# One load for the first 512 tokens, wider first matmuls and a new order of work in a gated attention + MLP kernel

## The chip, the core and the metric

The kernel runs on one core of a Trainium2 chip. A core has five engines that run at the same time and meet only at semaphores: TensorE (PE in the profile: matmuls; PEld: its weight loads), VectorE (DVE), ScalarE (ACT), GpSimd (POOL) and SyncE (SP), which here only issues transfers. Transfers between the chip's memory (HBM) and the core's on-chip memory (SBUF) run on 16 DMA engines; SP and ScalarE each put them into a queue of their own. TensorE writes to PSUM, eight banks of 128 partitions x 512 float32 columns.

The metric is the device time of one execution in microseconds (us).

## The reference

Input x has 2048 tokens of 512 features. The output is `g * a + (1 - g) * b` per token, where `g` is a sigmoid of x times a weight vector, `a` an attention branch and `b` an MLP branch:

```python
x = A_x
g = _sigmoid((x * gate_w).sum(-1, keepdims=True))
a = _A_ref(x, A_wq, A_wk, A_wv, A_wo, A_beta)   # 4 segments of 512 tokens, 32 heads of width 16
b = _B_ref(x, B_w_gate, B_w_up, B_w_down)       # (gelu(x w_gate) * (x w_up)) w_down, width 1792
return g * a + (1 - g) * b
```

In each segment the attention branch computes causal softmax attention within the segment, and reads a memory matrix that collects phi(k)^T v over the segments before it, with `phi(t) = t + 1 if t > 0 else exp(t)`. A sigmoid of beta mixes the two per head.

## The kernel before

**Tiling.** The four segments are called s = 0 to 3. For each, x is needed transposed (`xT`: four blocks of 128 features on the partitions, 512 tokens as columns), and from it come K and Q (four output blocks `K{s}_{t}`, `Q{s}_{t}`, each a sum over four feature blocks), V (four token tiles `V{s}_{tile}`), the MLP's gate (`G{s}_{ft}`, 14 blocks) and up projections (`U{s}_{ft}`, 14 blocks), attention scores (`qk...`, 20 steps with an exponential on ScalarE behind each), probabilities times V (`pv...`), and the down projection with the attention's output projection (`D...`, `R...`). A name such as `K0_2.1` is the second piece of a task's matmuls. Results leave PSUM by a copy on ScalarE or VectorE (`...ev`).

**Order.** Nothing is scheduled at run time. `ORDER` (L43) lists, for each of the five engines, every task in the order in which that engine issues it. `Sched.schedule` (L271) walks the lists with modelled durations to give PSUM banks to tasks; `LANDING` (L39) is the model's table of when each first transfer is there. `Emitter` then sets the semaphore waits that the data need. So each engine works strictly down its list: what waits there holds up all that stands behind it. That holds for SP's list of transfers too, and for the transfers that stand in ScalarE's list.

**The head, for segment 0.** Segments 1 to 3 get x transposed by the transfer itself (`xdma`, L594, four transposing loads per segment, named `x{s}_{kb}`). Segment 0 doesn't wait for that. Its x is loaded plain (`x0_0`, `x0_1`, L620) into the later buffer of the MLP's hidden values (`xin`, L613), transposed by TensorE against an identity (`x0t...`, L645), and copied from PSUM to `xT` on ScalarE (L652) or VectorE (L653). Before that, seven matmuls on constants (`warm0` to `warm6`, L636) keep TensorE at work while the first loads are under way.

The plain loads put tokens on partitions: a load of 256 tokens reads `(p a) d -> p a d`, so partition p holds two neighbouring tokens, one piece of 2 KB. The copy to `xT` sorts the columns back into token order. The two loads are u = 0 and u = 1, 256 tokens each. In `proj_T` (L715) the K matmuls of segment 0 are cut the same way, into two halves of 256 columns, so that the first half can start with `x0_0` alone; each K block is then eight matmuls instead of four.

**Loads in the head.** SP's list begins with `x0_0 x0_1 w_wk2 w_wq1 w_wv1 w_wg0 x1_0 ...`, ScalarE's with `tload w_wk0 w_wk1 w_wq0 w_wv0`. `wk` comes in three pieces (feature blocks 0, 1 and 2 to 3), `wq` and `wv` in two halves, the gate weights `wg` in two halves of 896 KB each.

**Gate logits.** For the sigmoid `g` of segment 0, x is multiplied by the weights in place (`gmul0`) and summed (`gsum0_a`); the sums stand in the order of the plain load and four small transfers (`gl...`, L820) bring them into the order of token tiles.

Of the kernel before, what the change touches and what calls it, by code (L numbers as in the profile page):

```python
# [1269 lines left out]
```

## Time and profile before

| | us |
|---|---|
| median of 3 runs | 261.96 (261.95 to 262.55) |
| the profiled execution | 261.81 |
| its span, first to last instruction | 260.6 |
| TensorE busy | 256.8 |
| ScalarE busy | 211.3 |
| VectorE busy | 186.6 |
| GpSimd busy | 105.9 |
| TensorE's first matmul of the projections starts | 4.75 |
| TensorE's first score step starts | 13.77 |

The profile comes from one execution. "Busy" for TensorE counts from the start of a matmul to its modelled end; matmuls overlap, so 16 in a row take less than 16 times the duration of one, and the distance between starts is the better price. A row of a timeline gives start, length, engine, line of the kernel, operation, tensors and count; in brackets stands idle time before it and what ended it. For a transfer, the row is its issue; "to landing" is counted from the start of the issue to the semaphore that says it is there. "SPq" and "ACTq" are the queues that issue.

### The profile page before, as it was taken

To read this page: it belongs to the slowest core of one execution; us is meant where nothing else is said; L and a number is where in the kernel's file an instruction comes from. 1 tells how busy PE (TensorE), PEld (TensorE's weight loads), DVE (VectorE), ACT (ScalarE), POOL (GpSimd) and SP (SyncE) were. 2 spreads that over 40 slices of the span, in tenths; PEclk is the share of its full clock that TensorE was granted. 3 is DMA by queue.
4 is the path that set the end of the run, shared out by engine and by line. 5 is a ranking of instruction groups with operands and counts; after the bars stand their busy time and mean duration, and the time that the engine had idled before them with its cause. 6 is when DMAs were issued, how large, how long until landed. Compare 5 with 4: busy or idle time off the path is not lost.

```text
span 260.6 us, 10413 instructions
## 1 busy us (share of the span) xinstructions
PE 256.8 (99%) x4670; PEld 127.1 (49%) x4670; DVE 186.6 (72%) x346; ACT 211.3 (81%) x191; POOL 105.9 (41%) x260
## 2 busy tenths in 40 slices
PE   8999999999999999999999999999999999999996
PEld 5544445345544664534454563454455445454454
DVE  2398889998998338898987217889898602688574
ACT  4699999999998887979868967889985878777721
POOL 8216766814006364263810251545280044327320
PEclk9999999999999999999999999999999999999999
DMA  7962211998012382060004023102001200420002
GB/s 217 315 177 42 51 38 45 253 356 162 3 23 56 45 110 63 9 118 3 3 3 103 3 64 71 34 4 87 0 6 23 81 5 0 92 77 3 3 3 83
DMA packets 33100, 18.43 MB, mean 71 GB/s; under 512 B 21152, under 2 KB 32800, under 8 KB 33056
## 3 DMA queue, kind: packets, MB, share of 16 engines
q1 hardware_dynamic: 32224, 16.99, 27.8%
q8 instruction: 36, 0.59, 0.9%
q10 hardware_dynamic: 832, 0.79, 0.9%
q14 instruction: 8, 0.07, 0.1%
HBM read 9.84 MB, written 2.10 MB: 46 GB/s over the span
## 4 chain that ended last, share of the span: by engine, by line
PE 96%; DMA 2%; ACT 1%; SPq 0%; issue 0%; DVE 0%
PE psW L543 36%; PE psW L545 26%; PE psW L1096 14%; PE psXALL L928 9%; PE psW L976 6%; DMA wk<-in_A_wk_dram 2%; PE psXALL L545 2%; PE psW L984 1%; PE psXALL L543 1%; ACT ptl L934 1%; PE psXALL L847 1%; PE psW L894 1%; SPq L580 0%; DVE obf L1162 0%
## 5 line engine op out<-in xcount | busy, mean ns | idle before, releaser
L934 ACT ACTIVATE pt<-psXALL 128x2048 bf16<-128x2048 f32 x64 | 120.1, 1877 | 24.5 <-PE psXALL L928 23.5
L937 POOL TENSOR_SCALAR_AFFINE_SELECT pt<-pt 128x256 bf16<-128x256 bf16 x128 | 56.1, 448 | 90.4 <-ACT pt L934 85.6
L937 POOL TENSOR_SCALAR_AFFINE_SELECT ptl<-ptl 128x512 bf16<-128x512 bf16 x32 | 23.9, 748 | 48.6 <-ACT ptl L934 47.0
L1075 DVE TENSOR_TENSOR hT<-psW,hT 128x512 bf16<-128x512 f32 x56 | 37.2, 684 | 8.8 <-PE psW L543 6.7
L1096 PE MATMUL psW<-wd,hT 32*128 32x512 bf16 x576 | 35.0, 374 | 0.0
L543 PE MATMUL psW<-xT,wg 128*128 128x512 bf16 x128 | 31.3, 380 | 0.0
L543 PE MATMUL psW<-xT,wu 128*128 128x512 bf16 x126 | 31.3, 380 | 0.0
L990 DVE STREAM_TRANSPOSE tb<-psW 128x512 f32<-128x512 f32 x32 | 22.3, 706 | 8.7 <-PE psW L984 8.5
L928 PE MATMUL psXALL<-qT,kpad 32*128 32x320 bf16 (+3 forms) x512 | 25.6, 272 | 0.2 <-ACT ptl L934 0.2
L545 PE MATMUL psW<-xT,wu 128*32 128x512 bf16 x392 | 24.6, 380 | 0.0
L1125 DVE TENSOR_SCALAR ost<-psW,omgt 128x512 bf16<-128x512 f32 x11 | 8.0, 746 | 23.1 <-PE psW L543 21.9
L1096 PEld LDWEIGHTS psW<-wd,hT 32*128 32x128 bf16 x576 | 18.8, 93 | 10.5
L545 PE MATMUL psW<-xT,wg 128*32 128x512 bf16 x384 | 22.9, 379 | 0.0
L1059 ACT ACTIVATE hT<-psW 128x512 bf16<-128x512 f32 x28 | 15.5, 597 | 7.3 <-PE psW L545 7.3
L928 PEld LDWEIGHTS psXALL<-qT,kpad 32*128 32x128 bf16 x512 | 8.6, 92 | 22.7 <-ACT pt L934 15.9
L976 PE MATMUL psW<-pt,vaug 128*17 128x192 bf16 (+3 forms) x512 | 19.3, 273 | 0.0
L543 PEld LDWEIGHTS psW<-xT,wg 128*128 128x128 bf16 x128 | 11.5, 98 | 14.4 <-issue 1.5
L543 PEld LDWEIGHTS psW<-xT,wu 128*128 128x128 bf16 x126 | 11.2, 98 | 14.3 <-issue 2.1
L976 PEld LDWEIGHTS psW<-pt,vaug 128*17 128x17 bf16 x512 | 12.2, 91 | 10.1 <-issue 0.6
L934 ACT ACTIVATE ptl<-psXALL 128x2048 bf16<-128x2048 f32 x8 | 15.0, 1877 | 1.6 <-PE psXALL L928 1.6
L834 POOL COPY exsT<-exs 32x4 f32<-32x4 f32 x64 | 14.0, 219 | 3.8
L545 PEld LDWEIGHTS psW<-xT,wu 128*32 128x32 bf16 x392 | 10.1, 97 | 9.5 <-issue 0.8
(126 smaller groups left out, 382.6 us busy)
## 6 DMA issues: line engine op xcount, KB each, us to landing
out_dram<-ost SPq DMA_DIRECT2D x15, 128.0 KB, 1.8
wg<-in_B_w_gate_dram SPq DMA_DIRECT2D x2, 896.0 KB, 7.5
wu<-in_B_w_up_dram SPq DMA_DIRECT2D x2, 896.0 KB, 6.8
wd<-in_B_w_down_dram SPq DMA_DIRECT2D x2, 896.0 KB, 7.6
phkt<-in_A_x_dram SPq DMA_DIRECT2D x3, 512.0 KB, 3.9
vlow<-vaug SPq DMA_DIRECT2D x8, 136.0 KB, 2.7
hT<-in_A_x_dram SPq DMA_DIRECT2D x2, 256.0 KB, 3.3
wo<-in_A_wo_dram SPq DMA_DIRECT2D x1, 512.0 KB, 6.0
```

The costliest lines, as they stand in the source:

```text
L543: return e.matmul(view(), lhsT, rhs, start=first, stop=last)
L545: r = e.matmul(view()[c:c + 32, :], lhsT[:, c:c + 32], rhs, start=first, stop=last, tile_position=(0, c))
L834: cross = task(f"exsT{s}", POOL, [Instr(lambda e, g=g, c=c: e.tensor_copy(exsT[sl][32 * g:32 * g + 32, c:16:4], exs[32 * c:32 * c + 32, s4 ...
L928: instrs.append(Instr(lambda e, g=g, lhs=lhs, rhs=rhs, c0=c0, ncol=ncol: e.matmul(X[g][:, c0:c0 + ncol], lhs(32 * g), rhs(32 * g), start=T ...
L934: exp_task(s, f"exp{s}_{t}{name}", [Instr(lambda e: e.activation(dst[:], XALL[:, :].rearrange("p (g c) -> p g c", g=4), ACTF.Exp, scale=AT ...
L937: task(f"msk{s}_{t}{name}", POOL, [Instr(lambda e, view=view, pat=pat, base=base: e.affine_select(out=view, in_=view, compare_op=ALU.is_ge ...
L976: instrs.append(Instr(lambda e, t=t, q=q, kb=kb, slot=slot, c0=c0: e.matmul(gp.f32()[32 * q:32 * q + 17, 128 * kb + 64:512], Vaug[sl][:, k ...
L990: task(f"pvt{s}_{t}_{j}", DVE, [Instr(lambda e: e.transpose(Tb[:, j, :], gp.f32()[:, :]), [gp.key], [("Tb", j)], 0.71)], grp=gp)
L1059: lambda e, g=g, ft=ft, s=s: e.activation(hT[s % 2][:, ft, :], g.f32()[:, :], ACTF.Gelu_apprx_tanh),
L1075: task(f"Um{s}_{ft}", DVE, [Instr(lambda e, g=g, ft=ft: e.tensor_tensor(hT[sl][:, ft, :], g.f32()[:, :], hT[sl][:, ft, :], ALU.mult), [g.k ...
L1096: return Instr(lambda e: e.matmul(gs[tile].f32()[:, :], a[32 * r:32 * r + 32, :], b[32 * r:32 * r + 32, :], start=False, stop=False, tile_ ...
L1125: DVE: [Instr(lambda e: e.tensor_scalar(ost[:], g.f32()[:, :], omgt[:, gt:gt + 1], None, ALU.mult), rd, wr, dve_t(512, ap=True))]}, grp=g))
```

## The change

Five things change together.

- **x0 in one load.** The two loads of 256 tokens become one of 512, four neighbouring tokens per partition, a piece of 4 KB each. The transposes are grouped by feature block (`x0t0`, `x0t1` for blocks 1 and 2, `x0t3`), each in two parts u for the token rows 0-1 and 2-3; block 3 goes to a rotating PSUM bank. The copies write every fourth token.
- **The first K in 512 columns.** `proj_T` no longer cuts segment 0's K, so each K block is four matmuls of 512 columns.
- **wk in four pieces.** Blocks 0 and 1 stay on ScalarE's queue, blocks 2 and 3 come on SP's.
- **The last warm-up matmul** has 256 columns instead of 512.
- **New orders for all engines,** and a new `LANDING` table. In SP's list the first half of `wg` now stands behind three transposing loads of x1 and two small loads; in ScalarE's list the first half of `wv` stands behind two copies of x0 and `K0_0even`. The gate logits' four transfers follow the new token order: each writes one column and needs all four sums.

```diff
 LANDING = {
-    "x0_0": 3.8, "w_wk0": 4.15, "x0_1": 5.2, "w_wk1": 5.7, "w_wk2": 6.6, "w_wq0": 7.0, "w_wq1": 8.4, "w_wv0": 9.2,
-    "w_wv1": 10.2, "w_wg0": 12.2, "x1_0": 12.9, "w_gwb": 13.2, "x1_1": 13.8, "w_beta": 14.1, "x1_2": 14.4, "x1_3": 14.8,
+    "x0_0": 3.5, "w_wk0": 4.0, "w_wk1": 4.4, "w_wk2": 4.7, "w_wk3": 5.0, "w_wq0": 6.0, "w_wq1": 7.2, "w_wv0": 8.0,
+    "w_wv1": 9.2, "w_wg0": 11.6, "x1_0": 12.3, "w_gwb": 12.8, "x1_1": 13.3, "w_beta": 13.7, "x1_2": 14.1, "x1_3": 14.6,
 }
 # ORDER, "pe" (TensorE)
-        "warm0 warm1 warm2 warm3 warm4 warm5 warm6 x0t0a_0 x0t0b_0 x0t1_0 K0_2.0 K0_3.0 K0_0.0 K0_1.0 x0t0a_1 x0t0b_1 "
-        "x0t1_1 K0_2.1 K0_3.1 K0_0.1 K0_1.1 K0_2.2 K0_3.2 K0_1.2 K0_0.2 K0_2.3 K0_1.3 K0_2.4 K0_0.3 K0_1.4 K0_2.5 "
-        "K0_0.4 K0_3.3 K0_3.4 K0_1.5 K0_0.5 K0_0.6 K0_2.6 K0_0.7 K0_1.6 K0_2.7 K0_1.7 Q0_3.0 Q0_0.0 Q0_1.0 Q0_1.2 "
-        "Q0_0.2 Q0_2.0 Q0_3.2 Q0_2.2 K0_3.5 K0_3.6 K0_3.7 G0_2.0 G0_3.0 qk0_0A0 G0_2.2 V0_2.0 V0_3.0 V0_3.2 V0_2.2 "
+        "warm0 warm1 warm2 warm3 warm4 warm5 warm6 x0t0_1 x0t1_1 x0t0_0 x0t3_0 x0t1_0 x0t3_1 K0_1.0 K0_3.0 K0_0.0 "
+        "K0_1.1 K0_1.2 K0_0.1 K0_0.2 K0_1.3 K0_0.3 Q0_3.0 Q0_1.0 Q0_2.0 Q0_0.0 Q0_2.2 Q0_1.2 Q0_3.2 Q0_0.2 K0_3.1 "
+        "K0_3.2 V0_1.0 K0_3.3 qk0_0A0 V0_2.0 V0_1.2 K0_2.0 V0_2.2 G0_3.0 K0_2.1 qk0_0B0 K0_2.2 Q1_0.0 Q1_0.2 K0_2.3 "
 ...
 # "act" (ScalarE)
-        "tload w_wk0 w_wk1 w_wq0 w_wv0 x0ev0b_0 x0ev0b_1 x0ev1_1 K0_0even K0_1ev K0_2ev kl0_01 pke0_0 Q0_1ev Q0_0ev "
+        "tload w_wk0 w_wk1 w_wq0 x0ev1_1 x0ev1_0 K0_0even w_wv0 K0_0ev pke0_0 Q0_2ev Q0_3ev Q0_0ev kl0_01 kl0_10 "
 ...
 # "dve" (VectorE)
-        "x0ev0a_0 x0ev1_0 x0ev0a_1 K0_0ev kp0_0 kl0_21 kp0_1 Q0_2ev gmul0 Gev0_2 gsum0_2 kl0_11 Vev0_2 kl0_00 gsum0_3 "
+        "x0ev0_1 x0ev0_0 x0ev3_0 x0ev3_1 K0_1ev kp0_1 Q0_1ev kl0_11 kp0_0 K0_3ev kl0_00 gmul0 Vev0_2 gsum0_3 gsum0_1 "
 ...
 # "sp" (the transfers that SP issues)
-        "x0_0 x0_1 w_wk2 w_wq1 w_wv1 w_wg0 x1_0 w_gwb x1_1 w_beta x1_2 x1_3 w_wg1 gl00 gl11 Vlo0_1 gl10 gl01 pkT0_1 "
+        "x0_0 w_wk2 w_wk3 w_wq1 w_wv1 x1_0 x1_2 x1_3 w_gwb w_beta w_wg0 x1_1 w_wg1 gl1 Vlo0_1 Vlo0_0 gl3 gl2 gl0 "
 ...
-    for u in range(2):
-        rank[0] -= 20000.0
-        dma(f"x0_{u}", SP, lambda u=u: xin[:, 2 * u:2 * u + 2, :],
-            lambda u=u: A_x[0, u * 256:(u + 1) * 256, :].rearrange("(p a) d -> p a d", p=P), [],
-            [("hT", 1, 2 * u + a) for a in range(2)], 250000, bias=rank[0], issue=0.5)
...
+    dma("x0_0", SP, lambda: xin, lambda: A_x[0, 0:512, :].rearrange("(p a) d -> p a d", p=P), [],
+        [("hT", 1, a) for a in range(4)], 500000, bias=rank[0], issue=0.5)
+    for wkey, i, dst, src in wloads:
+        wdma((wkey, i), SP if (wkey, i) in (("wk", 2), ("wk", 3), ("wq", 1), ("wv", 1)) else ACT, dst, src, 250000, issue=0.5)
 ...
+        n = 256 if i == 6 else 512
 ...
-    for nm, u, k0, nk, c0 in (("0a", 0, 0, 1, 0), ("0b", 0, 1, 1, 1024), ("1", 0, 2, 2, 2048),
-                              ("0a", 1, 0, 1, 3072), ("0b", 1, 1, 1, 1280), ("1", 1, 2, 2, 512)):
+    for nm, k0, nk, c0 in (("0", 0, 1, 0), ("1", 1, 2, 2048), ("3", 3, 1, None)):
 ...
-        dst = xT[0][:, k0:k0 + nk, 256 * u:256 * u + 256].rearrange("p k (c a) -> p k a c", a=2)
+            dst = xT[0][:, k0:k0 + nk, :].rearrange("p k (c a) -> p k a c", a=4)[:, :, 2 * u:2 * u + 2, :]
 ...
-        nu = 2 if head and wkey == "wk" else 1
-        cols = [slice(512 // nu * u, 512 // nu * (u + 1)) for u in range(nu)]
+        one = head and wkey == "wk"
+        wk_of = lambda kb: ("w", (wkey, kb if wkey == "wk" else kb // 2))
 ...
+        ins = [mm(g, view, w[:, kb, t * 128:(t + 1) * 128], xs[:, kb, :], [*xk(s, kb), wk_of(kb)],
+                  kb == 0, kb == 3, 512, fkey=key) for kb in range(4)]
 ...
-            for h in range(2):
-                for a in range(2):
-                    dma(f"gl{h}{a}", SP, lambda h=h, a=a: glog[a:P:2, h:4:2],
-                        lambda h=h, a=a: glog[64 * h:64 * h + 64, 12 + a:16:2],
-                        [gk + (c,) for c in (a, 2 + a)], [("glog", 0, h, a), ("glog", 0, 2 + h, a)], 60000, nonc=True)
+            for c in range(4):
+                dma(f"gl{c}", SP, lambda c=c: glog[:, c:c + 1],
+                    lambda c=c: glog[32 * c:32 * c + 32, 12:16],
+                    [gk + (a,) for a in range(4)], [("glog", 0, c)], 60000, nonc=True)
```

More of the change, by code (lines that the diff above doesn't have):

```diff
@@ L635, in _build @@
         gw = Grp(banks)
-        task(f"warm{i}", PE, [Instr(lambda e, gw=gw: e.matmul(
-            gw.f32()[:, :], ones[:, 0:128], ones[:, :], start=True, stop=True),
-            [], [gw.key], mm_t(512))], grp=gw, bias=5000.0 - i)
+        n = 256 if i == 6 else 512
+        task(f"warm{i}", PE, [Instr(lambda e, gw=gw, n=n: e.matmul(
+            gw.f32()[:, 0:n], ones[:, 0:128], ones[:, 0:n], start=True, stop=True),
+            [], [gw.key], mm_t(n))], grp=gw, bias=5000.0 - i)
     XB = XALL.bitcast(BF)
-    for nm, u, k0, nk, c0 in (("0a", 0, 0, 1, 0), ("0b", 0, 1, 1, 1024), ("1", 0, 2, 2, 2048),
-                              ("0a", 1, 0, 1, 3072), ("0b", 1, 1, 1, 1280), ("1", 1, 2, 2, 512)):
-        src = XB[:, c0:c0 + 256 * nk].rearrange("p (k c) -> p k c", c=256)
-        key = ("x0ps", c0)
-        keys = [key, ("x0ps", c0 // 1024 * 1024)] if c0 in (512, 1280) else [key]
-        task(f"x0t{nm}_{u}", PE, [Instr(lambda e, k=k, a=a, u=u, k0=k0, src=src: e.transpose(
-            src[:, k, a * 128:(a + 1) * 128], xin[:, 2 * u + a, (k0 + k) * 128:(k0 + k + 1) * 128],
-            ident[:, :]), [("hT", 1, 2 * u + a), ("c", "ident")], keys, mm_t(128))
-            for k in range(nk) for a in range(2)])
-        dst = xT[0][:, k0:k0 + nk, 256 * u:256 * u + 256].rearrange("p k (c a) -> p k a c", a=2)
-        wr = [("xT", 0, k0 + k, u) for k in range(nk)]
-        S.add(Task(f"x0ev{nm}_{u}", {
-            ACT: [Instr(lambda e, dst=dst, src=src: e.activation(dst, src.rearrange("p k (a c) -> p k a c", a=2), ACTF.Copy), [key], wr, act_t(256 * nk))],
-            DVE: [Instr(lambda e, dst=dst, src=src: e.tensor_copy(dst, src.rearrange("p k (a c) -> p k a c", a=2)), [key], wr, dve_t(256 * nk, 2))]}))
@@ new lines, in _build @@
+    for nm, k0, nk, c0 in (("0", 0, 1, 0), ("1", 1, 2, 2048), ("3", 3, 1, None)):
+        gx = Grp(banks) if c0 is None else None
+        for u in range(2):
+            if gx is None:
+                view = lambda c=c0 + 1024 * u, nk=nk: XB[:, c:c + 256 * nk].rearrange("p (k c) -> p k c", c=256)
+                key = ("x0ps", c0 + 1024 * u)
+            else:
+                view = lambda gx=gx, u=u: gx.f32().bitcast(BF)[:, 256 * u:256 * u + 256].rearrange(
+                    "p (k c) -> p k c", c=256)
+                key = gx.key
+            kw = {} if gx is None else {"grp": gx}
+            task(f"x0t{nm}_{u}", PE, [Instr(lambda e, k=k, a=a, u=u, k0=k0, view=view: e.transpose(
+                view()[:, k, a * 128:(a + 1) * 128], xin[:, 2 * u + a, (k0 + k) * 128:(k0 + k + 1) * 128],
+                ident[:, :]), [("hT", 1, 2 * u + a), ("c", "ident")], [key], mm_t(128))
+                for k in range(nk) for a in range(2)], **kw)
+        for u in range(2):
+            if gx is None:
+                view = lambda c=c0 + 1024 * u, nk=nk: XB[:, c:c + 256 * nk].rearrange("p (k c) -> p k c", c=256)
+                key = ("x0ps", c0 + 1024 * u)
+            else:
+                view = lambda gx=gx, u=u: gx.f32().bitcast(BF)[:, 256 * u:256 * u + 256].rearrange(
+                    "p (k c) -> p k c", c=256)
+                key = gx.key
+            kw = {} if gx is None else {"grp": gx}
+            dst = xT[0][:, k0:k0 + nk, :].rearrange("p k (c a) -> p k a c", a=4)[:, :, 2 * u:2 * u + 2, :]
+            wr = [("xT", 0, k0 + k, u) for k in range(nk)]
+            S.add(Task(f"x0ev{nm}_{u}", {
+                ACT: [Instr(lambda e, dst=dst, view=view: e.activation(
+                    dst, view().rearrange("p k (a c) -> p k a c", a=2), ACTF.Copy), [key], wr, act_t(256 * nk))],
+                DVE: [Instr(lambda e, dst=dst, view=view: e.tensor_copy(
+                    dst, view().rearrange("p k (a c) -> p k a c", a=2)), [key], wr, dve_t(256 * nk, 2))]}, **kw))
@@ L722, in proj_T @@
         xs = xT[s % NX]
-        nu = 2 if head and wkey == "wk" else 1
-        cols = [slice(512 // nu * u, 512 // nu * (u + 1)) for u in range(nu)]
-        wk_of = lambda kb: ("w", (wkey, min(kb, 2) if wkey == "wk" else kb // 2))
-        held = [("x0ps", c0) for c0 in ((0, 512), (1024, 1280), (2048,), (3072,))[t]] if x else []
-        ins = [mm(g, lambda c=c: view()[:, c], w[:, kb, t * 128:(t + 1) * 128], xs[:, kb, c],
-                            [*(xk(s, kb)[u:u + 1] if nu > 1 else xk(s, kb)), wk_of(kb)],
-                            (u, kb) == (0, 0), (u, kb) == (nu - 1, 3), 512 // nu, fkey=key)
-               for ks in ((0, 1), (2, 3)) for u, c in enumerate(cols) for kb in ks]
+        one = head and wkey == "wk"
+        wk_of = lambda kb: ("w", (wkey, kb if wkey == "wk" else kb // 2))
+        held = [("x0ps", c0) for c0 in ((0,), (1024,), (2048,), (3072,))[t]] if x else []
+        ins = [mm(g, view, w[:, kb, t * 128:(t + 1) * 128], xs[:, kb, :], [*xk(s, kb), wk_of(kb)],
+                  kb == 0, kb == 3, 512, fkey=key) for kb in range(4)]
         ins[0].writes += tuple(held)
-        pieces(name, g, ins, 1 if nu == 2 else 2)
+        pieces(name, g, ins, 1 if one else 2)
         if even is not None:
@@ L818, in prep @@
         if s == 0:
[L819 to L823 removed]
+            for c in range(4):
+                dma(f"gl{c}", SP, lambda c=c: glog[:, c:c + 1],
+                    lambda c=c: glog[32 * c:32 * c + 32, 12:16],
+                    [gk + (a,) for a in range(4)], [("glog", 0, c)], 60000, nonc=True)
         exp_task(ph, f"gexs{s}", [Instr(lambda e: e.activation(exs[:, s4], glog[:, s4], ACTF.Exp),
[L825 to L826 removed]
+                                        [("glog", s, a) for a in range(4)], [("exs", s)], 0.25)])
         task(f"gts{s}", DVE, [
```

7 lines of the change are left out of this document (1 added, 6 removed), and 153 rows, old and new, of the table ORDER.

## The prediction, made before the change was run

> **What bounds the kernel now.** I read the page's busy shares and its chain first, then the span cut by stages, then TensorE's own timeline in the head.
>
> ```profile
> span 260.6 us, 10413 instructions
> ...
> PE 256.8 (99%) x4670; PEld 127.1 (49%) x4670; DVE 186.6 (72%) x346; ACT 211.3 (81%) x191; POOL 105.9 (41%) x260
> ...
> PE 96%; DMA 2%; ACT 1%; SPq 0%; issue 0%; DVE 0%
> ```
>
> TensorE is busy all but 3.8 us, and the chain that ends last is 96% TensorE. So time is lost or won only where TensorE waits, or where it is given other work. The stages from 7.38 us on say where the 3.8 us don't lie:
>
> ```profile
> 7.38:12.81 5.43, 5.43 (x35) 3.33 (x36) 1.96 (x6) 3.85 (x7) 0.66 (x1) 1.00 1.16 314
> 12.81:250.00 237.19, 236.89 (x4357) 115.18 (x4358) 177.41 (x329) 203.06 (x178) 98.14 (x242) 1.00 0.27 61
> 250.00:260.60 10.60, 8.47 (x252) 5.14 (x244) 5.64 (x11) 1.40 (x3) 0.83 (x2) 1.00 0.16 51
> ```
>
> The first number behind each stretch is its length, the second TensorE's busy time; the last two are the busy share of the DMA engines and GB/s. From 12.81 to 250 us TensorE idles 0.30 us in all, so a new order there has next to nothing to win. The last stretch ends with the same four tasks in both orders. What is left is the head, up to 12.81 us:
>
> ```profile
> 0.85 3.15 PE L636 MATMUL psW<-const-bfloat16-1.0 128*128 128x512 bf16 x7 [0.85 <-PEq L1255]
> 3.79 1.01 PE L645 MATMUL psXALL<-ident,hT 128*128 128x128 bf16 x8
> 4.75 0.61 PE L543 MATMUL psW<-xT,wk 128*128 128x256 bf16 x4
> 5.20 0.61 PE L645 MATMUL psXALL<-ident,hT 128*128 128x128 bf16 x8
> 5.64 1.25 PE L543 MATMUL psW<-xT,wk 128*128 128x256 bf16 x10
> 7.38 1.81 PE L543 MATMUL psW<-xT,wk 128*128 128x256 bf16 x15 [0.48 <-DMA wk<-in_A_wk_dram]
> 9.03 3.62 PE L543 MATMUL psXALL<-xT,wq 128*128 128x512 bf16 x16
> 12.48 0.49 PE L543 MATMUL psW<-xT,wk 128*128 128x256 bf16 x3
> 12.81 1.03 PE L543 MATMUL psW<-xT,wg 128*128 128x512 bf16 x4
> 13.77 0.40 PE L928 MATMUL psXALL<-qT,kpad 32*128 32x448 bf16 x8
> ```
>
> The columns are start and length. Warm-up ends as the first half of x0 arrives; transposes and first K matmuls follow; the third piece of wk holds TensorE until 7.38; from there it is dense. At 12.81 all of K and Q of segment 0 (32 + 16 matmuls) is done: that is my mark for the comparison.
>
> **Part 1: 512-column K matmuls.** From the starts above, 15 matmuls of 256 columns take 9.03 - 7.38 = 1.65 us, 0.110 each; 16 of 512 columns take 12.48 - 9.03 = 3.45 us, 0.216 each. So 32 x 0.110 = 3.52 us become 16 x 0.216 = 3.46: 0.06 us won. The price is that each now needs both halves of x0 for its k-block, transposed and copied.
>
> **Part 2: x0 in one load.** TensorE's first transpose, now of the upper pair of token rows, waits for all 512 KB instead of 256.
>
> ```profile
> L580 SPq DMA_DIRECT2D hT<-in_A_x_dram x2: 387/397/407, 0.8 to 1.3; - x2
> ...
> DMA to landing us min/median/max: 2.9/3.3/3.6
> ```
>
> ```profile
> phkt<-in_A_x_dram SPq DMA_DIRECT2D x3, 512.0 KB, 3.9
> ```
>
> The two halves landed at 0.82 + 2.9 = 3.7 and 1.27 + 3.6 = 4.9 us. A 512-KB load of x on the same queue, in 1-KB rows, took 3.9 us: 0.82 + 3.9 = 4.7. The rate once running bounds it from below:
>
> ```profile
> 3.00:4.00 1.00, 1.00 (x5) 0.31 (x4) 0.00 (x0) 0.00 (x0) 1.00 (x1) 1.00 1.04 367
> 4.00:5.00 1.00, 1.00 (x11) 0.82 (x10) 0.60 (x2) 0.46 (x1) 1.00 (x2) 1.00 1.06 339
> ```
>
> At 340 to 367 GB/s, 256 KB more than the first half costs at least 0.7 us: 3.7 + 0.7 = 4.4 if the wk pieces of the other queue take nothing. Between 4.4 and 4.9 I take 4.5, near the lower end, because x0's packets are twice as large against wk's unchanged ones. The warm-up is half a matmul shorter and ends near 3.8, so TensorE idles some 0.7 us here. The Trainium skill's page "DMA: Bandwidth & Descriptors", section "Anatomy of one DMA — SWDGE (gpsimd) path", fits a GpSimd load by 2.0 us plus bytes over 436 GB/s, which as an estimate puts x0 at 4.0 us and the head 0.28 us earlier, the early-x0 rival below. The 3.9 us of this trace's 512-KB load is longer than the 3.2 of that fit, so the rows decide.
>
> **Part 3: from landing to the end of K and Q.**
>
> ```profile
> L645 PE MATMUL psXALL<-ident,hT x16: 219/241/314, 3.8 to 5.6; 128*128 128x128 bf16 x16
> ...
> L653 DVE COPY xT<-psXALL x3: 443/447/735, 4.3 to 5.5; 128x256 bf16<-128x256 bf16 x2, 128x512 bf16<-128x512 bf16 x1
> L652 ACT ACTIVATE xT<-psXALL x3: 456/457/734, 4.5 to 5.9; 128x256 bf16<-128x256 bf16 x2, 128x512 bf16<-128x512 bf16 x1
> ```
>
> Sixteen transposes stay, and six copies: four of 256 columns on VectorE, two of 512 on ScalarE. Call the landing L. The first k-block needs two VectorE copies in a row: two transposes 0.4, 2 x 0.45, 0.07 to the matmul: L + 1.37, when the transposes are over. Three K matmuls run to L + 2.02. The second k-block needs both ScalarE copies: six transposes 0.7, 2 x 0.735, 0.07: L + 2.27. Thirteen K and sixteen Q matmuls at 0.216 follow: L + 2.27 + 6.26 = L + 8.53, against 12.81. The balance is at L = 4.28; at L = 4.5 the head is 0.22 us later. Before, TensorE had stood still longer for wk, so most of the delay of x0 is covered.
>
> **Part 4: wk in four pieces.** The same 512 KB go in front of the same wq, and the pieces are needed at L + 1.4, 2.3, 2.5 and 3.1, the last at 7.6. The old third piece landed at 1.72 + 5.61 = 7.33:
>
> ```profile
> 1.72 5.61 DMA wk<-in_A_wk_dram
> ```
>
> The new fourth has no more bytes ahead of it on its queue (512 + 128 KB, before 512 KB and itself twice as long). No wait: 0. The cover is 0.3 us thick.
>
> **Part 5: SP's new order.** This is the step that I weigh most. Behind wv, SP issued wg's first half at 3.22; now three transposed loads of x1, gwb and beta go ahead of it. Issues on SP are in order and these are slow:
>
> ```profile
> 3.22 0.47 SPq L580 DMA_DIRECT2D wg<-in_B_w_gate_dram  x1
> 3.73 1.98 SPq L576 DMA_TRANSPOSE xT<-in_A_x_dram  x1
> 5.77 0.57 SPq L580 DMA_DIRECT2D gwb<-in_gate_w_dram  x1
> 6.38 2.40 SPq L576 DMA_TRANSPOSE xT<-in_A_x_dram  x1
> 8.83 0.58 SPq L580 DMA_DIRECT2D betab<-in_A_beta_dram  x1
> 9.46 3.36 SPq L576 DMA_TRANSPOSE xT<-in_A_x_dram  x2
> 12.86 0.58 SPq L580 DMA_DIRECT2D wg<-in_B_w_gate_dram  x1
> ```
>
> Three transposes: 1.98 + 3.36 and gaps, 3.22 to 8.6; gwb and beta 0.62 each; wg is issued at 9.85. Its landing behind transposes is the row of the second half:
>
> ```profile
> L580 SPq DMA_DIRECT2D wg<-in_B_w_gate_dram x1: 581/581/581, 12.9 to 12.9; - x1
> ...
> DMA to landing us min/median/max: 6.2/6.2/6.2
> ```
>
> By it wg lands at 16.05. From below: the 512-KB load's 3.9 us and 384 KB more at 367 GB/s, 1.07: 5.0, so 14.85. I take 15.0, near the lower end: transposes right ahead of wg delayed that row, and gwb and beta stand between here. The first gate matmul (G0_3.0) now stands behind 13 K, all 16 Q, 8 V matmuls and a score step, which takes 0.50 (13.77 + 0.40 less the 12.81 + 4 x 0.216 before it). That is L + 2.27 + 6 x 0.216 = L + 3.57 for the first nine K (K0_0.3 the last), 3.45 for Q, 0.86 for four K, 1.73 for V, 0.50: L + 10.1 = 14.6 at L = 4.5. Wait: 0.4 us. Behind it on TensorE stands everything, so nothing hides it. x1's second block is issued behind wg and needed 1.2 us after G0_3.0 starts; wg's second half is issued near 12.5 and needed 6 us after it: 0 for both.
>
> wv's first half moves on ScalarE's queue behind K0_0even, so its issue falls from 2.27 to about 8.4. It is needed at L + 3.57 + 3.45 + 0.43 = 12.0, 3.6 us later; 256 KB took 2.9 to 3.6 above. I take 0, and 0.4 as the upper end.
>
> **Part 6: the rest.** The gate logits' four small loads now each need all four sums. They feed one small ScalarE instruction that moves three ScalarE tasks back, so 0. For the orders behind 12.81 the bounds are -0.3 (the whole idle time) and, as the nearest row for a slip, one wait of 0.48; I take 0. Sum: +0.22 + 0.4 = +0.6 against the profiled run's 261.81 (span 260.6 and 1.2 around it), which is 0.15 below the median of 261.96. Forecast on the median's base: 261.96 + 0.62 = 262.6.
>
> **The rivals.** *wg's first half lands as late as the nearest row says* (slower): 16.05 against 14.6, a wait of 1.45 at G0_3.0, and with the 0.22 that is 263.6. It decides from a landing of 15.2 on (the balance L + 10.1 = 14.4 at L = 4.28, and 0.8 more). For it speaks that three transposes precede wg; against it that the queue has drained more by 9.85 than at 12.86. Chance 0.30, up to 264.3 if the three issues take 1.98, 2.40 and 1.68 (half of 3.36), 0.7 more.
>
> *TensorE stays at its slow rate* (slower): the seven warm-up matmuls took 3.15 us, 0.45 each against 0.216 later; the first eight transposes took 1.01 us and the second eight 0.61 (314 ns against 219 for one), and four K matmuls at 4.75 only 0.61. So the rate rose near 4.5 us, after 3.6 us of nearly unbroken work. Now a pause of 0.7 us lies in that stretch. If another 3.6 us is needed, counted from 4.5, K runs slow from 5.9 to 8.1, which loses 1.1 us: with the 0.22 that is 263.3, wg's wait then being covered. Against: the pause is short. Chance 0.12. The Trainium skill's page "TensorE: Matmul & The Clock Gate", section "What's actually happening", has the clock halved until an activity window of about 3.4 us was busy; by that rule the pause may spoil the window. The 4.5 us of this trace fits such a window, though the granted clock reads 1.00 throughout.
>
> *x0 lands early* (faster): at 4.0 the head gains 0.28, and if wg lands before 14.1 the time is 261.7; at 3.5, where the code's landing table has it, with wg by 13.6, 261.2. Against: 512 KB by 3.5 is less time than 256 KB took. Chance 0.13. That the change doesn't do what it says, with TensorE's wait for wk only moved to x0, is my forecast itself.
>
> **How the numbers follow.** Forecast 0.45 (262.0 to 262.9), late wg 0.30 (262.9 to 264.3), slow rate 0.12, early x0 0.13 (261.2 to 262.0). The range 261.4 to 264.2 leaves out the ends of the first and last. With 0.3%, or 0.79 us, as what a measurement can tell: faster 0.05 from early x0; slower 0.30 + 0.12 and 0.06 of the forecast's upper end; the rest the same.
>
> **What would show it.** The first transpose starts at 4.4 to 4.7 with x0's load named as its releaser. No wait for wk. K's 16 matmuls are 379 ns each. A wait of TensorE for wg of 0.2 to 0.8 us near 14.6, with wg issued at 9 to 10.5. I am wrong if x0 lands before 4.2, if wg is there in time, or if idle time over 0.8 us appears behind 17 us.

## The result: 9.6 us slower

The kernel after takes 271.5 us (median of 6, 270.6 to 272.08), the kernel before 261.86 beside it (261.57 to 262.55): ratio 1.0368 [1.0352, 1.0385]. The forecast was 262.6, with an upper end of 264.2. The profiled execution took 271.76 us, span 270.5. Ratios leave out executions over 1.5% above the fastest of the same kernel: two of e9's four and one of g3's four below. The page of the kernel after (busy shares, chain, granted clock in 40 slices):

```profile
span 270.5 us, 10147 instructions
...
PE 258.0 (95%) x4520; PEld 126.2 (47%) x4543; DVE 185.3 (68%) x344; ACT 214.6 (79%) x194; POOL 106.4 (39%) x260
...
PEclk9977999999999999999999999999999999999999
...
PE 75%; ACT 10%; DVE 7%; DMA 4%; issue 2%; DVEq 0%; ACTq 0%
```

The work on TensorE is the same, but its records show 12.5 us of idle time instead of 3.8. Some 3 us of that aren't idle: the trace has 4520 matmuls to 4543 weight loads, so 23 matmuls are missing from it, and most of the gaps behind 30 us are 0.2 us long, about the distance of one matmul from the next. That leaves some 6 us more than before. In slices 3 and 4 the granted clock (PEclk, the share of full speed that TensorE was given, in tenths) is down. TensorE's timeline from the landing of x0 on (start, length, engine, line, operation; in brackets idle time and what ended it):

```profile
4.79 1.03 PE L648 MATMUL psXALL<-ident,hT 128*128 128x128 bf16 x8 [1.00 <-DMA hT<-in_A_x_dram]
...
6.66 3.75 PE L543 MATMUL psW<-xT,wk 128*128 128x512 bf16 x9
10.24 3.62 PE L543 MATMUL psXALL<-xT,wq 128*128 128x512 bf16 x16
13.70 0.38 PE L543 MATMUL psW<-xT,wk 128*128 128x512 bf16 x1
18.48 1.03 PE L543 MATMUL psW<-wv,xT 128*128 128x512 bf16 x2 [4.41 <-DMA wv<-in_A_wv_dram]
```

One wait of 4.41 us for wv's first half stands where 0, at most 0.4, was forecast. Its origin is in the chain of waits (start, length, what) and in the transfers that SP issued:

```profile
0.82 3.92 DMA hT<-in_A_x_dram
...
10.44 0.02 ACTq L436
...
10.51 0.02 ACT kpad L745
10.53 7.91 DMA wv<-in_A_wv_dram
```

```profile
3.20 3.97 SPq L576 DMA_TRANSPOSE xT<-in_A_x_dram  x3
7.21 0.58 SPq L580 DMA_DIRECT2D gwb<-in_gate_w_dram  x1
7.83 0.43 SPq L580 DMA_DIRECT2D betab<-in_A_beta_dram  x1
8.30 0.43 SPq L580 DMA_DIRECT2D wg<-in_B_w_gate_dram  x1
8.78 1.23 SPq L576 DMA_TRANSPOSE xT<-in_A_x_dram  x1
10.06 0.59 SPq L580 DMA_DIRECT2D wg<-in_B_w_gate_dram  x1
```

The issue of wv stands behind `K0_0even` (kpad, L745), so it comes at 10.53, and the transfer then takes 7.9 us. SP's list puts both halves of wg, 1.8 MB, at 8.30 and 10.06. The stages by microsecond (length; busy time of PE, PEld, DVE, ACT, POOL; granted clock; DMA share; GB/s) show two more things:

```profile
10.00:11.00 1.00, 1.00 (x6) 0.48 (x5) 0.74 (x2) 0.49 (x1) 0.00 (x0) 1.00 0.08 17
11.00:12.00 1.00, 1.00 (x7) 0.42 (x5) 0.57 (x2) 0.94 (x3) 0.00 (x0) 1.00 0.19 46
12.00:13.00 1.00, 1.00 (x6) 0.46 (x5) 0.00 (x0) 1.00 (x2) 0.00 (x0) 1.00 0.81 294
...
16.00:17.00 1.00, 0.00 (x0) 0.00 (x0) 0.00 (x0) 0.00 (x0) 0.00 (x0) 0.80 1.05 365
17.00:18.00 1.00, 0.00 (x0) 0.00 (x0) 0.00 (x0) 0.00 (x0) 0.00 (x0) 0.50 1.07 368
...
22.00:23.00 1.00, 1.00 (x4) 0.34 (x3) 0.07 (x1) 1.00 (x2) 0.00 (x0) 0.50 0.00 0
23.00:24.00 1.00, 1.00 (x5) 0.33 (x3) 0.32 (x1) 0.01 (x1) 0.00 (x0) 0.79 0.00 0
```

From 10 to 12 us the DMA engines nearly stand still, although wg and the second small load had been issued. And TensorE's clock is halved in the wait: 0.80 from 16 to 17 (0.6 us at 1.00 and 0.4 at 0.50) puts the fall at 16.6, 2.5 us into the wait, and 0.79 from 23 to 24 puts the rise at 23.4, 4.9 us after the restart. Half rate for 4.9 us is, as an estimate, 2.5 us of work lost.

The copies of x0 are the last change in the head. They write every fourth token, two in a row on each engine:

```profile
5.65 2.46 ACT L664 ACTIVATE xT<-psXALL 128x512 bf16<-128x512 bf16 x2 [3.34 <-PE psXALL L648]
```

That is one per 1.23 us, where a copy of 512 columns to every second token took 0.734.

### The profile page after: what moved, and what is told of

It reads as the page before. It is cut to its first block, busy times and chain, and to the rows that moved or that the text cites. A ratio compares the mean times of both kernels' runs of the same rounds, so it can differ in the third digit from the quotient of the medians.

```text
span 270.5 us, 10147 instructions
## 1 busy us (share of the span) xinstructions
PE 258.0 (95%) x4520; PEld 126.2 (47%) x4543; DVE 185.3 (68%) x344; ACT 214.6 (79%) x194; POOL 106.4 (39%) x260
## 4 chain that ended last, share of the span: by engine, by line
PE 75%; ACT 10%; DVE 7%; DMA 4%; issue 2%; DVEq 0%; ACTq 0%
PE psW L543 31%; PE psW L545 16%; PE psW L1105 14%; PE psXALL L937 7%; ACT hT L1057 4%; PE psW L985 4%; DMA wv<-in_A_wv_dram 3%; ACT pt L943 3%; PE psXALL L545 1%; DMA hT<-in_A_x_dram 1%; DVE vaug L566 1%; PE psW L993 1%; ACT hT L563 1%; ACT ptl L943 1%; DVE hT L1084 1%
## 5 line engine op out<-in xcount | busy, mean ns | idle before, releaser
L946 POOL TENSOR_SCALAR_AFFINE_SELECT pt<-pt 128x256 bf16<-128x256 bf16 x128 | 56.8, 455 | 129.7 <-ACT pt L943 124.8
L543 PE MATMUL psW<-xT,wu 128*128 128x512 bf16 x145 | 36.1, 380 | 1.6 <-DVE hT L1084 0.6
L946 POOL TENSOR_SCALAR_AFFINE_SELECT ptl<-ptl 128x512 bf16<-128x512 bf16 x32 | 23.1, 723 | 18.5 <-ACT ptl L943 16.6
L545 PE MATMUL psW<-xT,wg 128*32 128x512 bf16 x456 | 27.4, 380 | 0.0
L543 PE MATMUL psW<-xT,wg 128*128 128x512 bf16 x105 | 25.4, 380 | 0.8 <-issue 0.6
L543 PEld LDWEIGHTS psW<-xT,wu 128*128 128x128 bf16 x154 | 13.9, 98 | 17.5 <-issue 1.9
L543 PE MATMUL psW<-wv,xT 128*128 128x512 bf16 x57 | 17.0, 414 | 4.6 <-DMA wv<-in_A_wv_dram 4.4
L545 PE MATMUL psW<-xT,wu 128*32 128x512 bf16 x280 | 18.6, 380 | 0.0
L985 PEld LDWEIGHTS psW<-pt,vaug 128*17 128x17 bf16 x512 | 12.4, 91 | 10.4 <-POOL pt L946 0.5
L843 POOL COPY exsT<-exs 32x4 f32<-32x4 f32 x64 | 15.2, 237 | 3.6
L543 PEld LDWEIGHTS psW<-xT,wg 128*128 128x128 bf16 x110 | 10.0, 99 | 12.9 <-issue 2.0
```

The lines of the kernel that those rows point to most:

```text
L543: return e.matmul(view(), lhsT, rhs, start=first, stop=last)
L545: r = e.matmul(view()[c:c + 32, :], lhsT[:, c:c + 32], rhs, start=first, stop=last, tile_position=(0, c))
L843: cross = task(f"exsT{s}", POOL, [Instr(lambda e, g=g, c=c: e.tensor_copy(exsT[sl][32 * g:32 * g + 32, c:16:4], exs[32 * c:32 * c + 32, s4 ...
L946: task(f"msk{s}_{t}{name}", POOL, [Instr(lambda e, view=view, pat=pat, base=base: e.affine_select(out=view, in_=view, compare_op=ALU.is_ge ...
L985: instrs.append(Instr(lambda e, t=t, q=q, kb=kb, slot=slot, c0=c0: e.matmul(gp.f32()[32 * q:32 * q + 17, 128 * kb + 64:512], Vaug[sl][:, k ...
```

## The experiments

All ratios are against the kernel before, run beside them.

### Is it the late issue of wv, or SP's order?

`e1`, the first half of wv moved back ahead of the copies:

```diff
-        "tload w_wk0 w_wk1 w_wq0 x0ev1_1 x0ev1_0 K0_0even w_wv0 K0_0ev ...
+        "tload w_wk0 w_wk1 w_wq0 w_wv0 x0ev1_1 x0ev1_0 K0_0even K0_0ev ...
```

> The changed kernel with one edit: ScalarE issues the first half of wv right behind wq again, before the copies of x0. Theory: the late wv cost 4.4 us of waiting and, through TensorE's slow rate after it, some 2.5 us more, while wg (landed at 15.8 us) is then needed at 16.5. Both go: 271.5 - 6.9 = 264.6 us (264.2 to 265.5), no slow clock in the rows. Rival: wg's first half or x1's second block takes over the wait, since their issue is as late as before: 267 us or more, with a wait of TensorE for wg or xT of over 2 us.

Measured: 265.24 (264.42 to 265.33), ratio 1.0119 [1.0098, 1.0141]. V starts at 13.75 with no wait, the clock stays at 1.00, and the wait for wg that the prediction had as its main term comes out, 0.42 us:

```profile
16.93 0.59 PE L543 MATMUL psW<-xT,wg 128*128 128x512 bf16 x2 [0.42 <-DMA wg<-in_B_w_gate_dram]
```

`e4`, SP's order alone put back, wv left late:

```diff
-        "x0_0 w_wk2 w_wk3 w_wq1 w_wv1 x1_0 x1_2 x1_3 w_gwb w_beta w_wg0 x1_1 w_wg1 ...
+        "x0_0 w_wk2 w_wk3 w_wq1 w_wv1 w_wg0 x1_0 w_gwb x1_1 w_beta x1_2 x1_3 w_wg1 ...
```

> The changed kernel with SP's old order of the first loads (wg's first half right behind wv, then x1, gwb, beta); the first half of wv stays behind K0_0even on ScalarE's queue. Theory: wv was late because both halves of wg and an x1 load had been issued just ahead of it; with wg moved by 11 us it lands some 4.3 us after its issue at 10.5, near 14.8: a wait of 0.7 us, no slow clock, 265.3 us. Rival: a load issued there takes about 8 us whatever stands on the other queue: wv lands after 17.5, 270 us or more.

Measured: 265.08 (264.65 to 265.23), 1.012 [1.0105, 1.0135]. In its timelines of ScalarE and TensorE wv is issued at almost the same time, but lands 3.7 us after its issue instead of 7.9, and V starts on it:

```profile
9.95 0.39 ACTq L580 DMA_DIRECT2D wv<-in_A_wv_dram  x1
```

```profile
13.71 0.60 PE L543 MATMUL psW<-wv,xT 128*128 128x512 bf16 x2
```

So neither edit alone does it. Either one put back takes away 2.5% (6.5 us), and that is measured. How it divides is an estimate: the wait of 4.41 and the 2.5 us at half rate, less the 0.42 for wg in e1, is 6.5; that leaves out that K also ended 0.4 to 0.6 us earlier in e1 and e4.

### Why does wv take 7.9 us behind SP's new order?

`e9` puts all transposing loads of x1 behind wg, `e10` puts wg's second half behind the first `gl` transfer, `e7` moves beta, `g3` both small loads:

```diff
 # SP's list after w_wv1: kernel after, e7, e9, e10, g3
-x1_0 x1_2 x1_3 w_gwb w_beta w_wg0 x1_1 w_wg1 gl1
+x1_0 x1_2 x1_3 w_gwb w_wg0 w_beta x1_1 w_wg1 gl1
+w_gwb w_beta w_wg0 w_wg1 x1_0 x1_2 x1_3 x1_1 gl1
+x1_0 x1_2 x1_3 w_gwb w_beta w_wg0 x1_1 gl1 w_wg1
+x1_0 x1_2 x1_3 w_wg0 x1_1 w_wg1 w_gwb w_beta gl1
```

> The changed kernel with one edit in SP's list: the load of beta (64 bytes for each partition) stands behind wg's first half instead of ahead of it. Theory: the 2 us around 10 to 12 us in which almost nothing moved belong to beta's load; wg's first half then starts near 10, lands near 13.7 instead of 15.8, and all that follows, wv's first half too, some 2 us earlier: 268 to 269 us. Rival: any plain load issued behind the transposing ones starts that late: wg lands near 15.8, wv near 18.4, 271.5 us.

Measured: 272.08 (271.67 to 272.71), 1.0394 [1.0373, 1.0416]: the rival's time. wg's first half landed at 15.0, 0.8 us earlier than in the kernel after, and a slow stretch of 115 to 150 GB/s came at 13 to 16 us. K ran at full rate here and wv was issued at 9.30, 1.2 us earlier than in the kernel after; it still landed at 18.4, and the wait grew by most of what the head had won:

```profile
18.42 1.03 PE L543 MATMUL psW<-wv,xT 128*128 128x512 bf16 x2 [5.35 <-DMA wv<-in_A_wv_dram]
```

> The kernel after with SP's three early transposing loads of x1 and the fourth put behind both halves of wg; wv's first half stays behind K0_0even on ScalarE's queue. Tells whether the transposing loads make the stretch of 10 to 12 us in which the transfers moved 17 and 46 GB/s. Theory that the idle stretch belongs to the plain loads behind transposing ones: no microsecond from 4 to 12 below 200 GB/s, wv lands at 12.5 to 14.5 (issue about 10), V starts at 13.7 to 14.3, and the time is 264.5 to 266, unless x1 comes late for the first Q of segment 1. Rival, that wv is late because it is issued late behind the halves of wg, which share the engines with it: with both halves of wg ahead of it wv lands at 17 or later again, and the time is 270 to 272.

Measured: 271.2 (267.81 to 272.43), 1.0291 [1.0244, 1.0339]. The rival held for wv: issued at 10.73 behind both halves of wg, it lands as late as ever, and the idle stretch is there with no transposing load ahead of it (30 GB/s from 8 to 9, and this row; wait in TensorE's timeline):

```profile
9.00:10.00 1.00, 1.00 (x4) 0.42 (x3) 0.00 (x0) 0.00 (x0) 0.00 (x0) 1.00 0.34 80
```

```profile
19.28 1.03 PE L543 MATMUL psW<-wv,xT 128*128 128x512 bf16 x2 [4.78 <-DMA wv<-in_A_wv_dram]
```

> The kernel after with wg's second half behind the first of the gate logits' transfers, so that it is issued at 20 us or later and shares nothing with wv. Theory that wv's first half was slow because wg's second half (896 KB) moved beside it: wv lands at 15.5 to 16.5 instead of 18.4 and V starts there, 2 to 3 us earlier (then the blocks of G that need the second half wait, so that the whole time says little). Rival, that the transfers stood still behind the transposing loads and that the second half costs wv nothing: wv lands at 18 to 18.5 as before.

Measured: 278.08 (277.42 to 279.71), 1.0655 [1.0623, 1.0688], the second half of wg being late for the G blocks. What it was run for: wv, issued at 10.52 as in the kernel after, lands 1.7 us earlier.

```profile
16.80 1.03 PE L543 MATMUL psW<-wv,xT 128*128 128x512 bf16 x2 [2.51 <-DMA wv<-in_A_wv_dram]
```

> The kernel after with gate_w and beta, the two small loads that are spread over the partitions, behind wg's second half on SP's queue; the three transposing loads of x1 stay ahead of wg, wv stays late on ScalarE's queue. Theory that the two small loads made the transfers stand still from 10 to 12 us: no microsecond from 9 to 14 below 150 GB/s, wg's first half lands at 12.5 to 13.5, wv at 15.5 to 16.5, and V starts there; 268 to 270 us. Rival, that any plain load behind a transposing one waits 2 us: the stretch below 100 GB/s stays at 10 to 12, wv lands at 18 or later, 270.5 to 272.

Measured: 268.4 (267.02 to 271.83), 1.0235 [1.0202, 1.0267]. The idle stretch is gone, and wv lands 1.6 us earlier although both halves of wg are still beside it:

```profile
10.00:11.00 1.00, 1.00 (x6) 0.49 (x5) 0.96 (x3) 0.92 (x2) 0.00 (x0) 1.00 0.95 355
11.00:12.00 1.00, 1.00 (x7) 0.45 (x5) 0.11 (x1) 0.97 (x2) 0.00 (x0) 1.00 1.05 377
```

```profile
16.85 0.60 PE L543 MATMUL psW<-wv,xT 128*128 128x512 bf16 x2 [3.02 <-DMA wv<-in_A_wv_dram]
```

So two things are shown to make wv late. The first is wg, issued ahead of it. In the kernel after, wg's halves were there at 15.8 and 19.4 (7.5 and 9.3 us after their issues), and wv at 18.4 between them. Without the second half (e10) wv landed at 16.7, with the first half there at 15.6; in e4, where the first half had landed at 10.7, wv took 3.7 us. The second is the two small loads: they hold up what follows them on SP's queue by some 2 us (in g3 wg's first half was there at 12.9), so that wg moves just when wv should. From 12.2 us on, wg's two halves, the last block of x1 and wv are 2.2 MB; at the 370 GB/s of the rows that is, as an estimate, 6 us, 18.2.

The transposing loads aren't the cause of the idle stretch (e9, g3). That they can't delay wv isn't shown: in e9 both halves of wg were there by 16.4, and in the 2.8 us until wv landed x1's transposing loads were still under way, at 99 to 192 GB/s. The Trainium skill's page "DMA: Bandwidth & Descriptors", section "Queues, rings and completion order", says that each DMA engine takes turns between the queues by packets. By that alone wv would get its share from 12.2 us on; the rows don't show it, since wv landed 2.6 us behind wg's first half. How the small loads hold up their queue, and why wv stands behind wg, no run shows.

### What does the wait cost beside its length?

`e2` fills it with 18 matmuls on constants (the task `keep`), whose result nobody reads:

```diff
-K0_3.2 V0_1.0 K0_3.3
+K0_3.2 keep V0_1.0 K0_3.3
```

> The changed kernel with 18 matmuls on constants (3.9 us) put into TensorE's list just before the first V matmul, so that TensorE works while it waits for wv. Theory: wv still lands near 18.4 us, but the clock stays at 1.00 and the 4.9 us at half rate behind the wait go: 271.5 - 2.5 = 269.0 us. Rival: the slow stretch costs nothing, because ScalarE and the loads set the pace there: 271.5 us.

Measured: 272.78 (271.38 to 273.43), 1.041 [1.0377, 1.0442]: a miss. The clock stays at 1.00, the segment's R block starts at 92.2 us instead of 94.1, but then TensorE stands still for nothing that the profile names, and by 137 us all but 0.2 of the gain is gone:

```profile
PE psXALL L940 <- issue: 1.4, 1, 1.4
```

TensorE's last matmuls start 0.2 us earlier than in the kernel after; that e2's span is 1.1 us longer comes from the last two stores, which took 3.2 and 2.9 us to land instead of 1.8 and 1.6. So the 2.5 us aren't confirmed in the whole time, though the 1.9 us won up to R speak against the rival. That a lower clock goes with a longer time is seen between executions of one kernel: three of g3 at a mean clock of 1.00 took 267.0, 267.8 and 269.0 us, one at 0.987 took 271.8; four of the kernel after at 0.987 took 271.3 to 272.1, two at 0.994 took 270.6 and 270.8. Their waits were not profiled, so this doesn't measure the price either.

### The head

`e3` is e1 with contiguous copies, which leave segment 0's tokens in the order of the load (as in e5b, f2 and g2), `e5` is e4 with nine warm-up matmuls of 512 columns, `e5b` both on e4, `f2` both on e4 with wv early.

```diff
-            dst = xT[0][:, k0:k0 + nk, :].rearrange("p k (c a) -> p k a c", a=4)[:, :, 2 * u:2 * u + 2, :]
+            dst = xT[0][:, k0:k0 + nk, 256 * u:256 * u + 256].rearrange("p k (a c) -> p k a c", a=2)
-    for i in range(7):
+    for i in range(9):
-        n = 256 if i == 6 else 512
+        n = 512
```

> As e1, and the six copies of x0 write neighbouring columns instead of every fourth one, so segment 0's tokens stand in another order and its part of the output is that of other tokens; load, transposes and matmuls stay. Theory: the copies went from 0.45 to 0.70 us (VectorE) and from 0.735 to 1.23 us (ScalarE) because of the stride of four, which starts the K matmuls late and breaks them up; back at the old lengths K and Q end 1.6 us earlier: 1.6 below e1, 263.0 us. Rival: the copies are slow for another reason (both engines read PSUM at once): the same time as e1.

Measured: 264.71 (264.58 to 266.62), 1.0126 [1.009, 1.0162]: a miss. The copies fell to 0.29 us (VectorE) and 0.60 (ScalarE), but the nine K matmuls had become bound by TensorE's slow rate: 634 ns each for those that start by 8.8 us, against 379 later. Little was left to win there.

> As e4 (265.1 us), and the warm-up is nine matmuls of 512 columns instead of six and a half, so that TensorE works until x0 lands near 4.6 us. Theory: the pause of 0.8 to 1.0 us before the first transpose kept TensorE at half rate until about 9 us (nine K matmuls took 3.35 us there instead of 9 x 0.216 = 1.94); without it the rate rises near 4.5 us as before the change. The strided copies still hold the second feature block until about 7.7, so Q starts near 9.0 instead of 9.67: 264.4 us. Rival: the rate does not hang on the pause: K unchanged, 265.1 us or, for the longer warm-up, later.

Measured: 264.82 (264.65 to 265.44), 1.0123 [1.0101, 1.0145]. Q starts at 8.94, as the theory has it, but the time hardly moves.

> As e5 with the contiguous copies of e3 (segment 0's tokens stand in another order, so its part of the output is that of other tokens). Theory: slow rate and slow copies hid each other, which is why e3 gained only 0.5 against e1; with both gone K starts near 5.9, runs dense, and Q starts near 7.9: 1.1 below e5, 263.3 us. Rival: something else, such as the last pieces of wk, holds K: less than 0.4 below e5.

Measured: 264.93 (264.68 to 267.72), 1.0144 [1.0091, 1.0196]: a miss. In e4, e5 and e5b the end of Q moves from 13.1 to 12.4 to 12.0, and V starts at 13.7 to 13.8 in all three, since wv lands there; e5b:

```profile
8.50 3.62 PE L543 MATMUL psXALL<-xT,wq 128*128 128x512 bf16 x16
11.95 0.59 PE L543 MATMUL psW<-xT,wk 128*128 128x512 bf16 x2
13.80 0.60 PE L543 MATMUL psW<-wv,xT 128*128 128x512 bf16 x2 [1.25 <-DMA wv<-in_A_wv_dram]
```

> The kernel after with all four things put right that the runs so far name: wv's first half ahead of the copies on ScalarE's queue, SP's old order, nine warm-up matmuls of 512 columns instead of seven, and contiguous copies of x0 (which keeps segment 0's tokens in the order of the load, so that part of the output is that of a permuted segment 0). With wv late, the same kernel took 264.93 and waited 1.25 us for wv at 13.8. Theory that this wait was all that hid the gain: 263.3 to 263.9, V at 12.5 to 12.9 with no wait, and what is left over the kernel before (1.5 to 2 us) is x0's later landing and the new order behind it. Rival: some other loss takes the place of the wait, 264.6 to 265.

Measured: 263.47 (262.76 to 264.0), 1.0074 [1.0055, 1.0093], as expected: no wait, and V even at 12.23.

`e6` tests the pause itself on the kernel before, with five warm-up matmuls instead of seven:

```diff
-    for i in range(7):
+    for i in range(5):
```

> The kernel before with five warm-up matmuls instead of seven, so that TensorE pauses for some 0.7 us until the first half of x0 lands at 3.7; nothing else is changed. Theory: this pause alone keeps the half rate until about 9 us, so the 15 K matmuls of 256 columns behind wk's last piece (from 7.38) run at 0.21 us each until then instead of 0.11: 0.8 us more, 262.7 us. Rival: the rate rises near 4.5 us all the same: 261.9 us.

Measured: 263.38 (262.48 to 263.64), 1.0059 [1.0038, 1.0081]. That is 1.5 us, twice what the theory had. In the profiled execution, the fastest of the five (262.48), the pause is 0.89 us, and K and Q end 0.66 us later than the 12.81 of the kernel before; where the other four lost 0.8 to 1.2 us more isn't on record:

```profile
4.03 1.03 PE L645 MATMUL psXALL<-ident,hT 128*128 128x128 bf16 x8 [0.89 <-DMA hT<-in_A_x_dram]
4.97 1.03 PE L543 MATMUL psW<-xT,wk 128*128 128x256 bf16 x4
```

Four K matmuls take 1.03 us here instead of 0.61. But a pause doesn't always do it: e7's head is that of the kernel after, and there the transposes were at full rate, with K's nine matmuls held by the strided copies alone:

```profile
4.66 0.62 PE L648 MATMUL psXALL<-ident,hT 128*128 128x128 bf16 x8 [0.96 <-DMA hT<-in_A_x_dram]
...
6.34 0.82 PE L543 MATMUL psW<-xT,wk 128*128 128x512 bf16 x3 [0.62 <-DVE xT L666]
7.72 1.47 PE L543 MATMUL psW<-xT,wk 128*128 128x512 bf16 x6 [0.55 <-ACT xT L664]
9.02 3.62 PE L543 MATMUL psXALL<-xT,wq 128*128 128x512 bf16 x16
```

By the durations in the profiles, full rate comes between 4 and 6.8 us where TensorE has no pause ahead of x0 (before, f1, e5, e5b, f2, g2), and between 7 and 10 us where it has one of 0.8 to 1.0 us (the kernel after, e1 to e4, e6, g1), save for e7, where it is there by 4.7.

### The parts of the change

`f1`: the kernel before with wk in four pieces. `g1`: the change's head with the old order of work behind it, on all engines. `g2`: g1 with nine warm-ups and contiguous copies, so f2's head with the old order.

```diff
 # f1, against the kernel before (and min(kb, 2) becomes kb, the fourth piece on SP behind the third)
-              for wkey, w, src, cuts in (("wk", wk, A_wk, (0, 1, 2, 4)), ("wq", wq, A_wq, (0, 2, 4)),
+              for wkey, w, src, cuts in (("wk", wk, A_wk, (0, 1, 2, 3, 4)), ("wq", wq, A_wq, (0, 2, 4)),
 # g1, TensorE's list against that of the kernel after; all lists go on as in the kernel before
-... K0_1.3 K0_0.3 Q0_3.0 Q0_1.0 Q0_2.0 Q0_0.0 Q0_2.2 Q0_1.2 Q0_3.2 Q0_0.2 K0_3.1 K0_3.2 V0_1.0 K0_3.3 qk0_0A0 V0_2.0 ...
+... K0_1.3 K0_0.3 K0_2.0 K0_2.1 K0_2.2 K0_2.3 Q0_3.0 Q0_0.0 Q0_1.0 Q0_1.2 Q0_0.2 Q0_2.0 Q0_3.2 Q0_2.2 K0_3.1 K0_3.2 K0_3.3 G0_2.0 G0_3.0 qk0_0A0 ...
```

> The kernel before with one part of the change alone: wk in four pieces, the fourth behind the third on SP's queue (32 K matmuls of 256 columns, both x0 loads, the old orders). Before, TensorE waited 0.48 us at 7.38 for the piece of 256 KB that holds feature blocks 2 and 3. Theory that this wait is a loss of its own: block 2 lands earlier, the wait goes or shrinks to 0.2, and the median falls by 0.2 to 0.5 us, to 261.3 to 261.7. Rival: the bytes ahead of block 3 are the same, so the wait only moves one matmul further and nothing is won (261.7 to 262.0). A third issue of 0.45 us on SP pushes wg's first half to 12.5, needed at 12.81: a wait of up to 0.4 there would eat the gain.

Measured: 261.89 (261.55 to 262.26), 1.0016 [1.0007, 1.0025]. The wait of 0.48 is gone and nothing is won: in the profile x0 lands later, the first K waits 0.20 for a copy, and K and Q end at 12.66 instead of 12.81.

> The kernel after with the order of work of the kernel before on all five engines: only the first 22 entries of TensorE's list, the copies of x0 and the five first transfers on SP are the change's own; from the rest of K on, everything stands as before (wv early, wg fifth on SP). So it is the change without its new order: one load of x0, 512-column matmuls, wk in four pieces. Theory that the head alone costs the restart at 4.7, the slow rate until about 9 and the strided copies: K and Q end at 13.9 to 14.4 instead of 12.81 and the median is 262.6 to 263.3, with no wait above 0.3 behind it. Rival, that the new order costs nothing and the head costs all of it: 264.5 to 265, as with wv early in the new order (265.2).

Measured: 263.98 (263.36 to 264.85), 1.0084 [1.0062, 1.0106], between the two expectations. K and Q end at 14.51, 1.70 us late, and the span is 2.0 longer: behind the head the old order loses 0.3.

```profile
6.70 3.88 PE L541 MATMUL psW<-xT,wk 128*128 128x512 bf16 x13
10.41 3.62 PE L541 MATMUL psXALL<-xT,wq 128*128 128x512 bf16 x16
13.87 0.81 PE L541 MATMUL psW<-xT,wk 128*128 128x512 bf16 x3
14.51 1.03 PE L541 MATMUL psW<-xT,wg 128*128 128x512 bf16 x4
```

> The same with nine warm-up matmuls of 512 columns and contiguous copies of x0 (segment 0's tokens stay in the order of the load, so that this part of the output is that of a permuted segment 0): the head of the kernel that took 263.47 with the new order. Theory that 1.5 to 1.7 us of what that one lost against the kernel before came from the new order: K and Q end at 13.1 to 13.5, 261.6 to 262.2. Rival, that the head's loss grows behind it whatever the order: 263 to 263.5.

Measured: 262.23 (261.9 to 262.89), 1.0016 [1.0004, 1.0028], just above its expectation. Against f2 the order is all that differs, and it is worth 0.58%, 1.5 us, with intervals apart. The R block of segment 0 by its line, in the kernel before, f2 and g2 (start and end behind the durations):

```profile
L1096 PE MATMUL psW<-wd,hT x192: 372/374/375, 84.5 to 97.3; 32*128 32x512 bf16 x192
```

```profile
L1105 PE MATMUL psW<-wd,hT x192: 374/374/375, 86.3 to 98.9; 32*128 32x512 bf16 x192
```

```profile
L1103 PE MATMUL psW<-wd,hT x192: 372/374/375, 85.4 to 98.2; 32*128 32x512 bf16 x192
```

With K and Q 0.50 us late in f2 (V at 12.23 and five K matmuls still to do, against 12.81) and 0.56 in g2, R starts 1.8 and 0.9 us late. Of f2's 1.3 us between the mark and R, its chain of waits shows this one, for nothing that the profile names:

```profile
62.73 0.74 issue
```

The other 0.6 us aren't put to any row. e4 has the same wait (0.65 at 64.23); e5 and e5b have hardly any there and start R 0.3 to 0.5 us earlier than e4. Its cause stays open.

## Why the prediction was wrong

**Where it failed.** The step is the last one of Part 5: "wv's first half ... issue falls from 2.27 to about 8.4 ... needed at L + 3.57 + 3.45 + 0.43 = 12.0, 3.6 us later; 256 KB took 2.9 to 3.6 above. I take 0, and 0.4 as the upper end." wv landed at 18.4, 6.4 us behind that need. The issue was 2.1 us later than forecast (10.53), because `K0_0even` waits for K, and K for the strided copies and the slow rate. The price was of x0's loads, into queues with little else, at the start; the prediction's own row for wk's third piece, also 256 KB, had 5.61 us, and from 8.4 that alone lands at 14.0. Here 1.8 MB of wg, put there by the same edit of SP's list, went ahead of it and beside it, and 7.9 us was measured. Both halves of Part 5 were priced as if the other weren't there. The halved clock behind the wait had no term at all.

**Part 2** was right: x0 landed at 4.74 (forecast 4.5, bounds 4.4 to 4.9).

**Part 3** was mis-sized. A pair of copies took 1.3 to 1.55 us on VectorE and 2.46 on ScalarE; the forecast was 0.90 and 1.47, from copies with half the spacing. In e7, where the rate was full, Q starts at 9.02 instead of the 8.2 that L + 3.57 gives from its own x0 landing at 4.6.

**The slow rate**, a rival with 0.12, happened. Its price was right: 1.1 us was forecast, and between e7 and the kernel after, Q's start differs by 10.24 - 9.02 = 1.2, of which 0.1 is x0's later landing. Counting on "the pause is short" was the error; e6 shows a like pause costing 0.7 us in the head of the kernel before, and 1.5 in its median. Of the 2.1 us that g1's head and the old order cost, 1.8 go with more warm-up and contiguous copies (g2).

**Part 1 and Part 4** held: 379 ns for a K matmul at full rate, no wait for wk. Part 5's wg was issued at 8.30 (forecast 9.85) and landed at 15.8, near the rival's 16.05; the wait of 0.42 shows only in e1. That it is the 0.4 of the forecast is luck: wg landed there at 16.8 and was needed at 16.5, 1.8 and 1.9 us later than forecast.

**Part 6** was wrong in its bound. "Idle 0.30 us in all, so a new order there has next to nothing to win" says nothing on what it can lose; taken as 0, at most 0.48, it cost 0.9 (e4 against g1, intervals touching) to 1.5 us (f2 against g2).

In sum: 6.5 us from wv, 0.9 to 1.5 from the order, 1.8 from the slow rate and the copies, 0.4 left in g2: 9.6 to 10.2, against 9.6 measured. No variant beat the kernel before.

## What to carry to other kernels

- Price a moved transfer by everything that is issued in the microseconds after it, on all queues, and by when its issue really comes: an issue behind a compute instruction inherits all that delays that instruction. Two moves that each cost little alone (e1, e4) can cost 6.5 us together.
- A wait of TensorE of 2.5 us or more can have a second price, half rate for 3.3 to 5.5 us behind it. And where a late load hides a slow head, mending the head shows nothing until the load is mended too (e5b against f2).
- A low idle time bounds what a new order can win, not what it can lose.
